# A dilated gated convolution on one core: the lower half of M3 split over taps 2 apart, gates of six classes, joint S and D differences

## The chip, the core and the metric

The kernel runs on one core of a Trainium2 chip. A core has a matrix engine (PE, its weight loads shown as PEld), a vector engine (DVE), a scalar engine (ACT), GpSimd (POOL) and a sync engine (SP) that here issues transfers. Each works off its own queue in order, and semaphores hold an instruction until what it needs is there. The metric is the device time of one execution in microseconds (us): 306.66 before, the median of 3 runs (306.5 to 307.13).

## The reference

x is 2 x 16000 x 144, w is 15 x 144 x 288, w_o is 144 x 144, all bf16. A causal convolution of 15 taps, 2 steps apart, gives 288 columns; tanh of the first 144 times the sigmoid of the others goes through w_o.

```python
def reference(x, w, w_o):
    B, T, D = x.shape
    K = w.shape[0]
    dil = 2
    pad = (K - 1) * dil
    xp = jnp.pad(x, ((0, 0), (pad, 0), (0, 0)))
    h = jnp.einsum('btc,cd->btd', xp[:, pad:pad + T, :], w[0])
    for i in range(1, K):
        off = pad - i * dil
        h = h + jnp.einsum('btc,cd->btd', xp[:, off:off + T, :], w[i])
    f = h[..., :D]; g = h[..., D:]
    z = jnp.tanh(f) * sigmoid(g)
    return z @ w_o
```

## The kernel before

**Tiling.** Both batches lie behind one another as 32,032 steps, cut into ten blocks of 3072 and one of 1536. A block holds two planes (even and odd steps) of 128 channels in `xn`; the 16 channels that are left, for eight taps, come through a buffer in DRAM (`rs`) as `rx`. A block of 3072 is worked in two units (r = 0 and 1), the last one in a single unit: 21 units. A unit covers 12 classes of 128 output positions; `y` holds 12 x 288 sums, `zs` their 12 x 144 gated values.

**A fast convolution.** The 15 taps are not summed one by one. From x, DVE forms sums and differences 8 positions apart (`S`, `D`) and 16 apart (`E`), and of these differences 4 and 2 apart (`S4`, `D4`, `E4`, `S2`, `D2`, `E2`, and `E42` of E4); `Sr`, `Dr`, `Er` are the same for `rx`. `derive` makes each of them with one subtraction or addition, into a tile of its own. They are the weights that PE loads (`stat` picks 128 positions of one); the taps, and sums of taps made at the start (`G`, `GN`, `H`, `PW`, `PX`, `WN`), are the moving operands of 288 columns. Four products m = 0 to 3 (M0 with S, M1 with D, M2 and M3 with E) are combined to the 12 classes.

**Steps of a unit.** An order written out by hand (the strings FIRST for unit 0, EVEN and ODD in turn for units 1 to 19, FINAL for unit 20) says in which order the steps are issued; each engine gets its own steps in that order, fixed by `K_`. The steps that the change and the prediction name:
- `V.m` (`pe_V`, 2 matmuls) opens a `px` tile of two banks, `Vk.m` copies its first bank to its second on ACT, `Vp.m` adds 2 matmuls to each. `C.m.b` copies a bank of it to a `py` bank.
- `X.m.b` and `Y.m.b` (`pe_A`) add 4 matmuls and one for the rest channels onto those banks, for m = 0 and 1; `tX`, `tY` (ACT, `scaled`) take them to `m0` and `m1`.
- `v.m` (ACT) takes the px bank pair of V.2 or V.3 to `v2` or `v3`.
- `A.2.1`, `A.2.0`, `A.3.1` (`A_common`, 2 matmuls) write one bank, `Ak` copies it to a second bank, `Ap.m.b2.b1` (`A_private`, 3 matmuls) adds to each, `At` (DVE) takes the banks to `y`. A.2.1 lies in a px tile, the other two in py banks.
- The lower half of M3 goes another way: `X.3.0` and `X.3.1` add 3 + 1 matmuls each onto V.3's px tile, and `tX.3` (DVE) takes it.
- On DVE, `P` adds m0 and m1 (once for each half b2), `U` adds v2 to P (once for each half), `u3` takes v3 from the upper half of P, `s` writes m0 - m1.
- Gates: `gt.c`, `gs.c` (ACT, tanh and sigmoid of four classes from class c = 0, 4, 8), `gm.c` (DVE) multiplies them into `zs`. gt.0 and gs.0 run in the next unit.
- `zT` (SP) transposes `zs` by a transfer, `po.g` (6 matmuls of 144 columns) multiplies by w_o, `o.g` (ACT) copies out, `ST` stores. `LD` and `LL` issue loads.
- S, D, S4, D4, S2, D2, Sr and Dr of the next block are made in ODD, the E's of the block in EVEN.

**Buffers.** PSUM holds 2 `px` tiles of two banks, 3 `py` banks and 1 `po` bank. `d_pool` (S and D) has two buffers, `e_pool` one, `zs` two. Line 203 of the profile is every DVE sum, 305 every matmul of `mm`, 448 the gates, 542 the plain copies on ACT, 556 `scaled`, 482 the copies of `o`.

Of the kernel before, what the change touches and what calls it, by code (L numbers as in the profile page):

```python
# [22 lines left out]
):  # L23

# [800 lines left out]
```

## Time and profile before

| what | value |
|---|---|
| the three runs | 306.5, 307.13, 306.66 us |
| the profiled execution | 306.78 us |
| its span, first to last instruction | 305.0 us |
| granted PE clock, mean | 0.996 |
| PE, PEld busy | 295.2, 283.2 us |
| DVE, ACT busy | 281.6, 274.5 us |
| DVE, ACT instructions | 478, 635 |
| moved by DMA | 39.71 MB, mean 130 GB/s |

The span is the time between the first and the last instruction of the profiled execution; the rest of its time lies around it. Busy time is the union of an engine's instructions. In the groups of instructions a row is: source line, engine, operation, out<-in, out<-in (partitions x elements, type), count | busy us, mean ns of one | idle us before them and who ended it. A timeline row is: start, length in us, engine, line, operation, count; an idle time before it stands in brackets. A chain row is: start, length, engine, tile, line, count. The whole chain before is PE for 85%.

### The profile page before, as it was taken

What the parts mean: (1) busy time and instruction counts of PE and PEld (TensorE: products, weight loads), DVE (VectorE), ACT (ScalarE), POOL (GpSimd) and SP (SyncE); (2) the same over time, 40 slices, a digit from 0 to 9 for tenths busy, and PEclk for the clock granted to TensorE, in tenths of its full rate; (3) what the DMA queues carried; (4) which work ended last, traced back from release to release, by engine and by line L of the source; (5) the groups of instructions that cost most, each with busy time, mean ns of one, the idle gap of its engine ahead of it and who ended that gap; (6) DMA issues with size and microseconds to landing.
All of it is one profiled execution on the core that took longest, in us unless ns stands there. A gap on an engine that the chain in (4) does not pass through costs nothing.

```text
span 305.0 us, 6949 instructions
## 1 busy us (share of the span) xinstructions
PE 295.2 (97%) x2613; PEld 283.2 (93%) x2613; DVE 281.6 (92%) x478; ACT 274.5 (90%) x635; POOL 31.1 (10%) x69
## 2 busy tenths in 40 slices
...
GB/s 195 132 90 221 42 155 122 103 122 169 166 62 130 177 149 116 148 207 91 146 210 87 159 133 130 136 131 165 105 163 139 160 66 140 160 36 78 98 89 80
DMA packets 175914, 39.71 MB, mean 130 GB/s; under 512 B 173128, under 2 KB 175688, under 8 KB 175880
## 3 DMA queue, kind: packets, MB, share of 16 engines
...
## 4 chain that ended last, share of the span: by engine, by line
PE 85%; DMA 6%; POOL 4%; DVE 3%; issue 1%; ACT 0%; POOLq 0%; DVEq 0%
PE px L305 47%; PE py L305 28%; PE po L305 10%; DMA rs<-wz 3%; DMA rx<-rs 2%; POOL Wr L284 2%; POOL rs L139 1%; DMA wo_ab<-in_w_o_dram 1%; POOL wo_ab L341 1%; DVE S L203 1%; DVE y L203 0%; PE py L516 0%; DVE D L203 0%; DVE z L203 0%; DVE Dr L203 0%
## 5 line engine op out<-in xcount | busy, mean ns | idle before, releaser
L305 PEld LDWEIGHTS <-E 128*128 128x128 bf16 x756 | 94.7, 141 | 1.3 <-issue 0.3
L305 PEld LDWEIGHTS <-D 128*128 128x128 bf16 x462 | 56.9, 138 | 1.3 <-DVE D L203 0.6
L305 PEld LDWEIGHTS <-S 128*128 128x128 bf16 x462 | 56.6, 138 | 1.4 <-issue 0.7
L305 PE MATMUL px<-H,E 128*128 128x288 bf16 x252 | 44.6, 286 | 0.1
L542 ACT COPY px<-px 128x288 f32<-128x288 f32 x105 | 42.5, 405 | 1.5 <-PE px L305 0.7
L448 ACT ACTIVATE th<-y 128x576 bf16<-128x576 bf16 x62 | 42.9, 692 | 0.9 <-DVE y L203 0.9
L448 ACT ACTIVATE sg<-y 128x576 bf16<-128x576 bf16 x62 | 42.8, 690 | 0.0
L305 PE MATMUL po<-wo_ab,zT 128*128 128x144 bf16 x468 | 42.0, 226 | 0.0
L482 ACT CAST os<-po 128x432 bf16<-128x432 f32 x77 | 40.5, 526 | 0.0
L542 ACT COPY py<-px 128x288 f32<-128x288 f32 x84 | 32.5, 396 | 6.7 <-DVE y L203 4.8
L305 PEld LDWEIGHTS <-zT 128*128 128x128 bf16 x480 | 35.6, 98 | 2.1
L203 DVE TENSOR_TENSOR E<-E 128x1536 bf16<-128x1536 bf16 (+5 forms) x33 | 36.7, 1140 | 0.3
L556 ACT ACTIVATE m<-py 128x288 bf16<-128x288 f32 x84 | 34.1, 421 | 1.1 <-PE py L305 1.1
L556 ACT ACTIVATE m<-px 128x576 bf16<-128x576 f32 x42 | 27.4, 652 | 4.7 <-PE px L305 4.4
L203 DVE TENSOR_TENSOR z<-th,sg 128x576 bf16<-128x576 bf16 x62 | 27.9, 452 | 1.2 <-ACT sg L448 1.2
L542 ACT CAST v<-px 128x576 bf16<-128x576 f32 x42 | 26.8, 637 | 1.7 <-PE px L305 1.5
L305 PE MATMUL px<-G,S 128*128 128x288 bf16 x168 | 27.5, 286 | 0.0
L305 PE MATMUL py<-GN,D 128*128 128x288 bf16 x168 | 27.5, 286 | 0.0
L305 PE MATMUL py<-GN,S 128*128 128x288 bf16 x168 | 27.4, 286 | 0.0
L305 PE MATMUL px<-G,D 128*128 128x288 bf16 x168 | 26.7, 286 | 0.0
L305 PEld LDWEIGHTS <-Er 128*128 128x128 bf16 x168 | 23.9, 142 | 0.2
L305 PE MATMUL py<-Wr,Er 128*128 128x288 bf16 x84 | 24.0, 286 | 0.0
...
## 6 DMA issues: line engine op xcount, KB each, us to landing
...
xn<-in_x_dram SPq DMA_TRANSPOSE x22
```

The lines of the kernel that those rows point to most:

```text
L139: K_(eng.dma_start(out=bass.AP(o.tensor, o.offset, [[8 * CR, n], [1, 8 * CR]]), in_=wz[0:n, 0:8 * CR]))
L203: return K_(nc.vector.tensor_tensor(out=out_, in0=a, in1=b, op=op))
L284: K_(nc.gpsimd.dma_start(out=Wr[CR * k:CR * (k + 1), 2 + t // 8, :], in_=w[t, CM:D, :]))
L305: K_(nc.tensor.matmul(ps, lhsT=l, rhs=r, start=start and k == 0, stop=stop and k == n - 1, skip_group_check=not start))
L341: K_(nc.gpsimd.memset(wo_ab[:], 0.0))
L448: K_(nc.scalar.activation(out=cur["g", c0][k][:, 0:n], in_=cur["y"][:, c0:c0 + n, D * k:D * k + D], func=(ACT.Tanh, ACT.Sigmoid)[k]))
L482: K_(nc.scalar.copy(out=dst, in_=po[:, 0:n * D]))
L542: K_(nc.scalar.copy(out=dst, in_=src))
L556: K_(nc.scalar.activation(out=dst, in_=ps, func=ACT.Copy, scale=0.5))
```

## The change

M3's lower half gets steps like the other three halves of M2 and M3: `A.3.0` (2 matmuls with the new sum `NX` and `WN[5]`) into a px tile, `Ak.3.0`, `Ap.3.0.0` (1 + 1 matmuls), `Ap.3.0.1` (2 + 1), and `At.3.0` takes `P[0]` less the tile. `E42` is made two positions wider (16). `u3q` takes v3 from both halves of P. FIRST and FINAL keep X.3. Gates cover classes 0 to 5 and 6 to 11 (FINAL's own stay at four), so gt.6, gs.6, gm.6 stand for the steps of 4 and 8; gm.6 runs in the next unit. S and D share one tile, likewise S4 with D4 and S2 with D2; in ODD one subtraction makes S4 and D4 (`SD4`) and one S2 and D2 (`SD2`). P and U are one operation for both halves, U and u3q with v2 or v3 read twice (`twice`), but not in FINAL. The `ze` tiles move to a pool of their own, NX is made in FIRST (`wx`). All four orders are written anew.

```diff
     GEO = {"S": (-8, 16), "D": (-8, 16), "E": (-16, 24), "S4": (-8, 12), "D4": (-8, 12), "E4": (-16, 20),
-           "S2": (-4, 6), "D2": (-4, 6), "E2": (-12, 12), "E42": (-12, 14), "Sr": (0, 8), "Dr": (0, 8), "Er": (-8, 16)}
+           "S2": (-4, 6), "D2": (-4, 6), "E2": (-12, 12), "E42": (-14, 16), "Sr": (0, 8), "Dr": (0, 8), "Er": (-8, 16)}
...
+    def half_tile(cur, nm):
+
+        wd = GEO[nm][1]
+        if nm[0] == "E" or nm[-1] == "r":
+            cur[nm] = ((e_pool if nm[0] == "E" else d_pool).tile([P, wd * P], BF16, name=nm), 0)
+        elif nm not in cur:
+            t_ = d_pool.tile([P, 2 * wd * P], BF16, name="SD" + nm[1:])
+            cur["S" + nm[1:]], cur["D" + nm[1:]] = (t_, 0), (t_, wd * P)
+        return cur[nm]
...
+        if nm in ("SD2", "SD4"):
+
+            st = int(nm[-1])
+            u0, wd = GEO["S" + nm[-1]]
+            b0, bw = GEO["S"]
+            t_, o = half_tile(cur, "S" + nm[-1])[0], u0 - b0
+            b = cur["S"][0]
+            if big:
+                d_in, d_out = [[bw, 2 * P], [1, wd]], [[1, 2 * P * wd]]
+            else:
+                d_in, d_out = [[bw * P, 2], [1, wd * rw]], [[wd * P, 2], [1, wd * rw]]
+                o, st = o * rw, st * rw
+            tt(sub(t_, 0, d_out), sub(b, o + st, d_in), sub(b, o, d_in), ALU.subtract)
+            return
...
+    def neg_sum():
+        tt(NX[:], WN[:, 4, :], w_all[:, 14, :], ALU.subtract)
...
-    def gate_act(cur, c0, k, n=4):
+    def gate_act(cur, c0, k):
         if cur is None:
             return
+        n = 6 if c0 in (0, 6) else 4
         if k == 0:
-            cur["g", c0] = [g_pool.tile([P, 4, D], BF16, name=nm) for nm in ("th", "sg")] + [n]
+            cur["g", c0] = [g_pool.tile([P, 6, D], BF16, name=nm) for nm in ("th", "sg")] + [n]
         K_(nc.scalar.activation(out=cur["g", c0][k][:, 0:n], in_=cur["y"][:, c0:c0 + n, D * k:D * k + D],
                                 func=(ACT.Tanh, ACT.Sigmoid)[k]))
...
+    def twice(t_):
+
+        return sub(t_, 0, [[0, 2], [1, 2 * D2]])
+
+    def add_P(cur, b2=None):
+
+        k = slice(0, 2) if b2 is None else b2
+        tt(cur["P"][:, k], cur[0, "q"][:, k], cur[1, "q"][:, k], ALU.add)
+
+    def add_U(cur, b2=None):
+
+        if b2 is None:
+            both = [[2 * D2, 2], [1, 2 * D2]]
+            tt(sub(cur["U2"], 0, both), sub(cur["P"], 0, both), twice(cur["v2"]), ALU.add)
+        else:
+            tt(cur["U2"][:, b2], cur["P"][:, b2], cur["v2"][:], ALU.add)
...
+    def sub_v3(cur, both=False):
+
+        if both:
+            p = sub(cur["P"], 0, [[2 * D2, 2], [1, 2 * D2]])
+            tt(p, p, twice(cur["v3"]), ALU.subtract)
+            return
         tt(cur["P"][:, 1], cur["P"][:, 1], cur["v3"][:], ALU.subtract)
...
-    AC = {(2, 1): ("PW", 0), (2, 0): ("PW", 2), (3, 1): ("PX", 0)}
+    AC = {(2, 1): [PW[:, 0, :], PW[:, 1, :]], (2, 0): [PW[:, 2, :], PW[:, 3, :]], (3, 1): [PX[:, 0, :], PX[:, 1, :]],
+          (3, 0): [NX[:], WN[:, 5, :]]}
+
+    AP_ = {(2, 1): ([PW[:, 4, :], PW[:, 5, :]], [w_all[:, 0, :], w_all[:, 1, :]]),
+           (2, 0): ([w_all[:, 6, :], w_all[:, 7, :]], [WN[:, 0, :], WN[:, 1, :]]),
+           (3, 1): ([WN[:, 2, :], WN[:, 3, :]], [w_all[:, 8, :], w_all[:, 9, :]]),
+           (3, 0): ([w_all[:, 14, :]], [WN[:, 4, :], WN[:, 5, :]])}
...
     def A_common(cur, m, b2):
-        wt, k = {"PW": PW, "PX": PX}[AC[m, b2][0]], AC[m, b2][1]
-        if (m, b2) == (2, 1):
+        if (m, b2) in ((2, 1), (3, 0)):
             ps = cur["A", m, b2] = x_bank()
             b0, b1 = ps[:, 0, 0:D2], ps[:, 1, 0:D2]
         else:
             cur["A", m, b2] = (y_bank(), y_bank())
             b0, b1 = (t[:, 0:D2] for t in cur["A", m, b2])
         cur["Ab", m, b2] = (b0, b1)
-        mm(b0, [(stat(cur, "E4", SH[m] - (0 if b2 else 4) - j), wt[:, k + j, :]) for j in range(2)], True)
+        mm(b0, [(stat(cur, "E4", SH[m] - (0 if b2 else 4) - j), wt) for j, wt in enumerate(AC[m, b2])], True)
...
     def A_private(cur, m, b2, b1):
-        jobs = []
-        for j in range(2):
-            if m == 3:
-                wt = w_all[:, 8 + j, :] if b1 else WN[:, 2 + j, :]
-            elif b1:
-                wt = w_all[:, j, :] if b2 else WN[:, j, :]
-            else:
-                wt = PW[:, 4 + j, :] if b2 else w_all[:, 6 + j, :]
-            jobs.append((stat(cur, "E42", SH[m] - (0 if b2 else 4) - j - (0 if b1 else 2)), wt))
+        jobs = [(stat(cur, "E42", SH[m] - (0 if b2 else 4) - j - (0 if b1 else 2)), wt) for j, wt in enumerate(AP_[m, b2][b1])]
         jobs.append((stat(cur, "Er", SH[m] + 2 * b1 + 4 * b2), Wr[:, m, :]))
         mm(cur["Ab", m, b2][b1], jobs, False)
...
         if (m, b2) == (2, 1):
             tt(y[:, 10:12, :], u2[:, 1], cur["A", 2, 1][:, :, 0:D2], ALU.add)
+        elif (m, b2) == (3, 0):
+            tt(y[:, 0:2, :], cur["P"][:, 0], cur["A", 3, 0][:, :, 0:D2], ALU.subtract)
...
     FIRST = """
-        B wn0.0 wn0.1 wd.1 wd.0 wh.1 wh.0 S D S2 D2 S4 E D4 E2 Sr Dr E4 Er E42 w.0 z.9 wt.0 V.0 z.3 z.5 w.1 wt.1 Vk.0 V.1 z.12 z.7
-        w.2 wt.2 Vk.1 Vp.0 C.0.0 w.3 z.1 wt.3 Vp.1 wn w.8 C.0.1 wt.8 Y.0.0.main z.10 z.15 C.1.0 w.9 Y.0.1.main wt.9 X.1.0.main w.4
-        Y.1.0.main wt.4 X.0.1.main Y.0.0.rest tY.0.0 C.1.1 X.0.0.main w.5 X.0.1.rest Y.0.1.rest Y.1.0.rest X.0.0.rest wt.5 tX.0
-        tY.0.1 X.1.0.rest X.1.1 tX.1 w.6 V.2 Vk.2 Y.1.1 tY.1.0 A.2.1 Ak.2.1 tY.1.1 Vp.2 A.2.0 v.2 wt.6 Ak.2.0 Ap.2.1.0 Ap.2.1.1 V.3
-        Vk.3 P.1 s P.0 U.1 At.2.1 U.0 w.7 gt.4 wt.7 Ap.2.0.0 Vp.3 Ap.2.0.1 v.3 gs.4 At.2.0.0 A.3.1 V.0.n Vk.0.n X.3.0 X.3.1 At.2.0.1
-        u3 gm.4 tX.3 Ak.3.1 Vp.0.n Ap.3.1.0 At.3.1.0 Ap.3.1.1 At.3.1.1 gt.8 C.0.0.n gs.8 C.0.1.n
+        B wn0.0 wn0.1 wd.1 wd.0 wh.1 wh.0 S D S2 S4 D2 E D4 E2 Sr Dr E4 Er E42 w.0 wt.0 z.15 V.0 w.1 z.3 z.9 z.1 z.5 V.1 Vk.0 wt.1
+        w.2 Vk.1 wt.2 Vp.0 w.3 Vp.1 z.12 C.0.1 wt.3 w.8 C.0.0 Y.0.1.main X.0.0.main wn wt.8 w.9 z.10 z.7 wt.9 C.1.0 Y.0.0.main w.4
+        X.0.1.main wt.4 X.1.0.main w.5 Y.0.0.rest Y.1.0.main wt.5 tY.0.0 C.1.1 w.6 X.0.0.rest X.0.1.rest Y.1.0.rest X.1.0.rest X.1.1
+        Y.0.1.rest wt.6 tX.0 V.2 tY.1.0 Y.1.1 tX.1 Vk.2 tY.0.1 A.2.1 Vp.2 A.2.0 tY.1.1 Ak.2.1 v.2 Ak.2.0 P U w.7 Ap.2.1.0 V.3 Vk.3
+        wt.7 Ap.2.1.1 Ap.2.0.1 At.2.1 Vp.3 Ap.2.0.0 v.3 V.0.n A.3.1 Vk.0.n X.3.0 X.3.1 s At.2.0.0 At.2.0.1 Ak.3.1 Vp.0.n Ap.3.1.0
+        Ap.3.1.1 gt.6 C.0.0.n wx u3 tX.3 At.3.1.0 C.0.1.n gs.6 At.3.1.1
     """
     EVEN = """
-        B Y.0.0 V.1 X.0.0 po.1 X.0.1 gt.0 tY.0.0 Vk.1 Vp.1 Y.0.1 gs.0 o.1 po.2 C.1.0 Y.1.0 tX.0 C.1.1 o.2 E V.2 X.1.1 X.1.0 tY.0.1
-        Vk.2 tY.1.0 tX.1 gm.8.p Er gm.0 E2 E4 E42 P.1 zT LD Vp.2 v.2 Y.1.1 A.2.1 A.2.0 V.3 po.3 tY.1.1 Ak.2.1 s U.1 P.0 Ap.2.1.0
-        Ap.2.1.1 At.2.1 U.0 Ak.2.0 Vk.3 Vp.3 o.3 gt.4 v.3 gs.4 u3 Ap.2.0.0 Ap.2.0.1 At.2.0.0 A.3.1 V.0.n Vk.0.n X.3.1 X.3.0 At.2.0.1
-        gm.4 tX.3 Ak.3.1 Vp.0.n Ap.3.1.0 Ap.3.1.1 At.3.1.0 At.3.1.1 ST LL po.0 gt.8 C.0.0.n C.0.1.n o.0 gs.8
+        B Y.0.0 V.1 Vk.1 tY.0.0 gt.0 X.0.1 X.0.0 Vp.1 po.1 Y.0.1 C.1.0 tX.0 C.1.1 E Y.1.0 X.1.1 V.2 X.1.0 o.1 tY.1.0 gs.0 tY.0.1 Vk.2
+        tX.1 Y.1.1 Er E4 E2 gm.6.p A.2.0 Vp.2 po.2 A.2.1 gm.0 E42 zT LD tY.1.1 P Ak.2.0 v.2 Ak.2.1 U A.3.1 Ap.2.0.0 V.3 Ap.2.1.1
+        Ap.2.1.0 At.2.0.0 At.2.1 s Vk.3 o.2 Vp.3 v.3 po.3 Ap.2.0.1 A.3.0 V.0.n At.2.0.1 u3q Ak.3.1 o.3 Vk.0.n Ak.3.0 gt.6 ST LL
+        Ap.3.1.1 Ap.3.1.0 Vp.0.n Ap.3.0.0 Ap.3.0.1 po.0 At.3.1.0 At.3.1.1 At.3.0 C.0.0.n C.0.1.n gs.6 o.0
     """
     ODD = """
-        B D Y.0.0 X.0.1 po.1 V.1 X.0.0 gt.0 Vk.1 tY.0.0 D2 Vp.1 Y.0.1 tX.0 C.1.0 V.2 Y.1.0 C.1.1 gs.0 o.1 tY.0.1 tY.1.0 Vk.2 Dr
-        gm.8.p X.1.0 X.1.1 Y.1.1 A.2.0 tX.1 tY.1.1 Ak.2.0 Vp.2 v.2 A.2.1 po.2 Ap.2.0.1 Ak.2.1 V.3 Ap.2.1.0 Ap.2.1.1 S D4 S4 gm.0 Sr
-        zT LD P.1 P.0 s o.2 Vk.3 Vp.3 gt.4 v.3 gs.4 U.1 U.0 At.2.1 Ap.2.0.0 At.2.0.0 S2 A.3.1 V.0.n po.3 Vk.0.n X.3.0 X.3.1 Vp.0.n
-        gm.4 At.2.0.1 u3 Ak.3.1 o.3 Ap.3.1.0 Ap.3.1.1 gt.8 ST LL po.0 tX.3 At.3.1.0 At.3.1.1 C.0.0.n gs.8 C.0.1.n o.0
+        B D Y.0.0 X.0.0 X.0.1 V.1 Y.0.1 gt.0 Vk.1 tX.0 tY.0.0 Vp.1 po.1 C.1.0 C.1.1 V.2 Y.1.0 gs.0 Vk.2 o.1 tY.0.1 S Dr X.1.1 X.1.0
+        Y.1.1 Vp.2 tY.1.0 tX.1 tY.1.1 v.2 po.2 A.2.1 A.2.0 Ak.2.1 Ak.2.0 o.2 A.3.1 V.3 Ap.2.1.0 Vk.3 Ap.2.1.1 Ap.2.0.0 Vp.3 Ap.2.0.1
+        Sr SD4 gm.0 SD2 gm.6.p zT LD P U At.2.1 At.2.0.0 A.3.0 po.3 v.3 Ak.3.0 Ak.3.1 V.0.n Ap.3.0.1 s At.2.0.1 u3q Vk.0.n o.3 gt.6
+        ST LL Ap.3.1.0 Ap.3.0.0 Vp.0.n Ap.3.1.1 po.0 At.3.1.0 At.3.0 At.3.1.1 C.0.0.n C.0.1.n gs.6 o.0
     """
...
     FINAL = """
-        B V.1 Y.0.0 Vk.1 gt.0 X.0.1 po.1 Vp.1 gs.0 tY.0.0 C.1.0 X.0.0 Y.0.1 Y.1.0 tX.0 C.1.1 tY.1.0 o.1 E V.2 X.1.0 X.1.1 tY.0.1 Vk.2
-        tX.1 po.2 o.2 E4 E2 E42 gm.8.p gm.0 Er Vp.2 v.2 Y.1.1 A.2.1 tY.1.1 Ak.2.1 A.2.0 V.3 po.3 Vk.3 P.1 s.1 Ap.2.1.1 Ap.2.1.0 Vp.3
-        U.1 s.0 P.0 U.0 o.3 Ak.2.0 Ap.2.0.0 gt.4 v.3 gs.4 At.2.1 At.2.0.0 Ap.2.0.1 At.2.0.1 gt.8 zT q.0 A.3.1 Ak.3.1 gs.8 X.3.0 X.3.1
-        ev.p0.V gm.4 u3 eB tX.3 q.1 Ap.3.1.0 At.3.1.0 gm.8 Ap.3.1.1 At.3.1.1 x6 eT.A eT.B ev.p1.A gp.0.2.1 gp.0.2.0 mh.0 ec.A eT.C
-        gp.2.1.0 gp.2.1.1 gp.3.1.1 gp.3.1.0 mh.1 ec.B e3.4 eT.D e3.7 ec.C ev.p2.A ev.p3.A e3.10 e2.0 ec.D ev.c4.V ev.c7.A ev.c10.A
-        e2.2 ev.c0.V ev.c2.A ST sp.0 sp.1 s4 LD s0
+        B V.1 Y.0.0 X.0.1 Y.0.1 Vk.1 Vp.1 X.0.0 gt.0 tY.0.0 C.1.0 tY.0.1 tX.0 C.1.1 po.1 Y.1.0 gs.0 tY.1.0 E V.2 X.1.0 X.1.1 Y.1.1
+        o.1 Vk.2 tX.1 tY.1.1 E4 E2 Er Vp.2 v.2 A.2.1 A.2.0 po.2 Ak.2.0 V.3 Ak.2.1 Vk.3 E42 gm.6.p gm.0 Ap.2.0.0 Ap.2.1.0 Vp.3
+        Ap.2.1.1 s.1 P.1 s.0 P.0 gt.4 o.2 v.3 U.1 U.0 At.2.0.0 At.2.1 Ap.2.0.1 po.3 A.3.1 X.3.1 X.3.0 gs.4 o.3 Ak.3.1 At.2.0.1 gt.8
+        gm.4 u3 tX.3 eB gs.8 Ap.3.1.0 At.3.1.0 zT LD q.0 Ap.3.1.1 ev.p0.V At.3.1.1 x6 q.1 eT.A gp.0.2.1 gp.2.1.1 gp.0.2.0 gp.2.1.0
+        gp.3.1.0 gp.3.1.1 ev.p1.A gm.8 eT.B mh.0 eT.C ec.A mh.1 ec.B eT.D e3.4 e3.7 ev.p2.V ec.C ev.p3.A ec.D ev.c4.V ev.c7.A e3.10
+        e2.0 e2.2 ev.c10.A ev.c2.A ev.c0.A ST sp.0 sp.1 s4 s0
     """
```

`AP_` gives the same weights as the old code for the old three halves; `stat` and the rest of `derive` add the offset of the half tile. The orders name `P`, `U`, `u3q`, `SD2`, `SD4`, `wx` without change to `step` beyond their entries.

More of the change, by code (lines that the diff above doesn't have):

```diff
@@ L71 @@
     g_pool = ctx.enter_context(tc.tile_pool(name="g", bufs=2))
+    ze_pool = ctx.enter_context(tc.tile_pool(name="ze", bufs=1))
     zt_pool = ctx.enter_context(tc.tile_pool(name="zt", bufs=2))
@@ L245, in derive @@
             x_ = x_[:].rearrange("p e c -> p (e c)")
-        o = t_[:, 0:wd * rw]
+        o = t_[:, t0:t0 + wd * rw]
         if big:
@@ L257, in stat @@
         blk, r = cur["blk"], cur["r"]
-        t_ = blk[nm]
+        t_, t0 = blk[nm]
         k = u - u0
@@ L263, in stat @@
             rw = 2 * (BTOK[blk["bi"]] // 48)
-            return t_[:, k * rw:(k + 2) * rw]
-        return t_[:].rearrange("p (n j) -> p n j", j=wd)[:, :, k + r]
+            return t_[:, t0 + k * rw:t0 + (k + 2) * rw]
+        return t_[:, t0:t0 + wd * P].rearrange("p (n j) -> p n j", j=wd)[:, :, k + r]
     ident = const.tile([P, P], BF16)
@@ L294 @@
     PX = const.tile([CM, 2, D2], BF16)
+    NX = const.tile([CM, D2], BF16)
     def x_bank():
@@ L637, in end_step @@
             c["os"] = os_pool.tile([P, NCL, D], BF16, name="os")
-            c["g", 0] = [g_pool.tile([P, 4, D], BF16, name=nm) for nm in ("th", "sg")] + [4]
+            c["g", 0] = [g_pool.tile([P, 6, D], BF16, name=nm) for nm in ("th", "sg")] + [4]
         elif op == "gp":
```

24 lines of the change are left out of this document (9 added, 15 removed).

## The prediction

> **What bounds the kernel now.** First the busy times, then the same in stretches of 10 us (columns: PE, PEld, DVE, ACT, POOL busy, clock, DMA share, GB/s):
>
> ```profile
> PE 295.2 (97%) x2613; PEld 283.2 (93%) x2613; DVE 281.6 (92%) x478; ACT 274.5 (90%) x635; POOL 31.1 (10%) x69
> ...
> 150.00:160.00 10.00, 10.00 (x92) 9.95 (x91) 9.78 (x17) 9.49 (x23) 0.00 (x0) 1.00 0.97 180
> ```
>
> Three engines look full, PE wholly so, at full clock. Busy time does not tell which one sets the pace, so I take the distance between starts. From the chain of waits, then the timeline:
>
> ```profile
> 126.61 1.96 PE px L305 x16
> ...
> 153.17 1.96 PE px L305 x16
> ```
> ```profile
> 156.32 0.54 PE L305 MATMUL po<-wo_ab,zT 128*128 128x144 bf16 x6
> ...
> 156.69 0.41 PE L305 MATMUL px<-PW,E 128*128 128x288 bf16 x2
> ```
>
> The same place of an even unit comes back after 26.56 us, the time of two units (one EVEN, one ODD). 1.96/16 = 0.1225 us is the step of a matmul of 288 columns; (156.69 - 156.32)/6 = 0.062 that of one of 144. The code gives a unit 96 wide matmuls (V 8, Vp 16, Y 20, X 28, A 6, Ap 18) and 24 narrow: 96 x 0.1225 + 24 x 0.062 = 13.24 us, twice 26.48. So PE stands still for 0.08 us in 26.56: its queue sets the pace in units 1 to 20.
>
> DVE is less full than 98%. From its timeline:
>
> ```profile
> 148.65 1.75 DVE L203 TENSOR_TENSOR E<-xn 128x3072 bf16<-128x3072 bf16 x1
> 150.32 0.45 DVE L203 TENSOR_TENSOR z<-th,sg 128x576 bf16<-128x576 bf16 x1
> 150.69 1.22 DVE L203 TENSOR_TENSOR Er<-rx 128x2048 bf16<-128x2048 bf16 x1
> ```
>
> A queued instruction starts about 0.08 us before the end of the one ahead (148.65 + 1.75 - 150.32). ACT does the same by about 0.10 (a v copy at 158.12 takes 0.64, the next gate starts at 158.66).
>
> **The change, part by part.** Rows used (busy, mean ns of one):
>
> ```profile
> L448 ACT ACTIVATE th<-y 128x576 bf16<-128x576 bf16 x62 | 42.9, 692 | 0.9 <-DVE y L203 0.9
> L542 ACT COPY px<-px 128x288 f32<-128x288 f32 x105 | 42.5, 405 | 1.5 <-PE px L305 0.7
> L203 DVE TENSOR_TENSOR z<-th,sg 128x576 bf16<-128x576 bf16 x62 | 27.9, 452 | 1.2 <-ACT sg L448 1.2
> L203 DVE TENSOR_TENSOR E<-xn 128x3072 bf16<-128x3072 bf16 x10 | 17.5, 1752 | 0.0
> L203 DVE TENSOR_TENSOR y<-m,m 128x1152 bf16<-128x1152 bf16 x20 | 15.1, 753 | 1.2 <-ACT m L556 0.2
> L203 DVE TENSOR_TENSOR E<-E 128x1536 bf16<-128x1536 bf16 x10 | 9.8, 983 | 0.0
> L203 DVE TENSOR_TENSOR S<-S 128x1536 bf16<-128x1536 bf16 x10 | 9.5, 950 | 0.0
> L203 DVE TENSOR_TENSOR S<-S 128x768 bf16<-128x768 bf16 x11 | 7.1, 643 | 0.0
> ```
>
> *PE.* X.3.0 and X.3.1 (2 x 4 matmuls) go; A.3.0 (2), Ap.3.0.0 (2) and Ap.3.0.1 (3) come: 8 - 7 = 1 wide matmul less, in EVEN and ODD alone (FIRST and FINAL keep X.3), so in 19 units: 19 x 0.1225 = **2.33 us** on the bounding queue.
>
> *ACT per unit.* Six gates of 0.69 (4.15) become four over 864 elements. None is in the trace; from 144, 288 and 576 elements (305, 434, 692 ns) the slope is 0.9 ns per element, so 0.94 each, 3.76 in all; bounds 0.90 and 1.04 (1.5 x 0.692). New: Ak.3.0, a copy of 0.405. Net +0.02, and one instruction less to overlap (+0.10): 29 instructions that fill 12.0 us of 13.28 (durations 14.9 less 29 x 0.10) become 12.1 of a unit of 13.12. Hidden under PE.
>
> *DVE per pair of units.* S4 and D4: 2 x 0.950 become one of 3072 elements, 1.752: -0.15. S2 and D2: 2 x 0.644 become 1536 in runs of 6, 0.983: -0.31. E42 grows from 1792 to 2048 elements, 1.093 to 1.220: +0.13. z: six of 0.452 become four of 0.604 (row GN of 864): -0.30. P and U: 0.904 become 0.753 each, four times: -0.60. u3 takes both halves, 0.454 to 0.753, twice: +0.60. Sum -0.63 in durations; but 8 instructions fewer lose 8 x 0.08 = 0.64 of overlap. Nothing: about 25.4 us (durations 28.9 less 43 x 0.08) before and after, against 26.56 before and 26.24 after.
>
> Joint U and joint u3 read v2 or v3 twice through a step of 0. No row has such an operand. Lower bound 0.753 (1152 elements); upper 1.35, the element rate of y<-P,px (576 in 750 ns) doubled. I take 0.753: like that row, all operands are two-byte with neighbours side by side.
> [...]
>
> *Queues.* SP and POOL issue the same transfers in the same order. zT in ODD waits for gm.6.p: from the start of the unit 0.6 (end of the last y) + S, D 2.28 + Dr, Sr 1.21 + SD4 1.67 + two z 1.04 + SD2 0.90 = 7.7 us, where z was complete at 6.4 (168.04 against the unit's 161.7). po.0 reads it at 12.75.
>
> *px banks.* Two tiles, until now five takers in a unit (V.1, V.2, A.2.1, V.3, V.0.n), now six: A.3.0 waits for At.2.1 (DVE), the next V.1 for At.3.0. Places on an unstalled PE queue, counted in matmuls: ODD A.3.0 at 10.05, At.2.1 ends 0.6 + the 7.1 to the second z + P, U 1.34 + 0.75 = 9.8. EVEN: A.3.0 at 10.42; At.2.1 follows Ap.2.1.0 (its end 9.4) and ends 10.14. Room 0.25 and 0.28. E42 ends 7.4 into EVEN, Ap.2.0.0 loads it at 7.7. Cost nothing, with 0.3 us of cover.
>
> *Head.* FIRST has the same matmuls. Joint P and U save DVE 0.13, NX adds one 128x288 (0.3, late), E42 +0.13, one z moves to unit 1: -0.2 or so, while unit 1 of before stands still for 1.06 us (from 29.04 to 42.23, less 96 x 0.1225 and one po). I take 0, bounds -1.1 (all of that filled) and +0.7 (Dr, which waits for rx to 31.6, now has Sr, SD4 and SD2 behind it). *Tail.* Same matmuls; two last os copies change engine: 0, bounds -0.3 and +0.3.
>
> **Sum.** -2.33 on PE. Stalls were 0.04 a unit; with cover down to 0.3 I let them grow by 0.02: +0.4. Head and tail 0. So -1.95. The profiled execution took 306.78 (span 305.0 and 1.78 around it), 0.12 over the median: 306.78 - 1.95 - 0.12 = **304.7 us**.
>
> **Rivals.**
>
> 1. *px bank* (slower). At.2.1 comes late each unit, A.3.0 and all PE work behind it stand. The head of before shows this wait, at V.0.n:
>
> ```profile
> 39.41 0.41 PE L305 MATMUL px<-H,S 128*128 128x288 bf16 x2 [0.35 <-DVE y L203]
> ```
>
> At 0.35 in every unit: 19 x 0.35 = +6.65, less 2.33: 311.0. It decides once At.2.1 is later than the room of 0.25 by more than 0.12, the matmul saved. For: DVE's free time falls from 1.1 to 0.8 us a pair, and U now waits for both halves. Against: y<-m,m and, in ODD, S2 no longer run ahead of At.2.1.
>
> 2. *Gate in front of the copies* (no change). gt.0 of six classes (0.25 longer) stands ahead of C.1.0, tX.0 and C.1.1 in EVEN; adding ACT's steps, C.1.1 ends at 4.1 and X.1.1, which overwrites what it copies, comes at 4.17. Room 0.1. A wait of 0.23 per EVEN unit eats the gain (10 x 0.23): 306.7. Against: ACT has 1 us a unit to catch up.
>
> 3. *zT late in ODD* (slower). From 7.7 to 12.75 are 5.0 us, before 6.4; 5.8 (36.02 to 41.85) is the shortest seen. DMA after the issue at 168.11, in 40 slices from 165 to 176:
>
> ```profile
> DMA  0000000000000001999999997799299999999996
> GB/s 0 0 0 0 0 0 0 0 0 0 0 0 0 0 0 32 213 215 204 220 214 219 171 175 114 158 244 215 20 202 287 281 278 149 101 196 291 288 103 38
> ```
>
> Data flows 1 us after the issue; 0.46 MB at 210 GB/s are 2.2: landed after some 3.4. Late by 0.6 in ten ODD units: 10 x 0.6 - 2.33 = +3.7: 310.3.
>
> 4. *Repeated operand at half rate* (slower). U and u3 at 1.35: +2.4 per pair, DVE needs 27.8 and paces: 9.5 x (27.8 - 26.56) = +11.8: 318.5.
>
> **How the numbers follow.** Forecast 0.75, px bank 0.09, gates 0.09, zT 0.04, half rate 0.03. By less than 0.2% (0.6 us) nothing can be told from no change. Faster 0.75, same 0.09, slower 0.16. The forecast's own range: 304.7 - 1.1 (head) = 303.6 to 306.0 (stalls of 0.07 more a unit). The range takes in the gates' case and a mild px wait (half of saved matmul and room lost): **303.6 to 307.2**; beyond it stay 0.16 above and a few hundredths below.
>
> **What would show it.** Right: the pair at 26.2 to 26.35 us; 19 matmuls fewer; U and P at 0.75; gates of 864 at 0.94; joint differences at 1.75 and 0.98; no PE idle before A.3.0 and X.1.1. Wrong: PE px idle <-DVE y at A.3.0 (rival 1), <-ACT at X.1.1 (2), po <-DMA zT (3), U at 1.35 (4), or unit 1 longer than 13.2 us.

## The result, and the profile after

The changed kernel takes 309.84 us, the median of 6 runs (309.07 to 310.33), against 306.91 for the kernel before on the same chip (6 runs, 306.5 to 307.29): a ratio of 1.0091 [1.0074, 1.0108], slower by 0.9%. The profiled execution took 309.88 with a span of 308.1, at a granted PE clock of 0.995; before it was 306.78, 305.0 and 0.996, so the clock explains nothing.

The busy times of the changed kernel, then the first 10 us of the same stretch as before (columns as before), then the chain of waits at an even unit:

```profile
PE 296.0 (96%) x2594; PEld 281.6 (91%) x2594; DVE 282.4 (92%) x399; ACT 272.8 (89%) x614; POOL 32.2 (10%) x69
```
```profile
150.00:160.00 10.00, 10.00 (x93) 9.89 (x90) 9.79 (x12) 9.55 (x23) 0.00 (x0) 1.00 1.18 141
```
```profile
124.32 1.96 PE px L331 x16
...
151.17 1.96 PE px L331 x16
...
177.83 1.96 PE px L331 x16
```

The matmuls are 2613 - 2594 = 19 fewer, as the change says. Busy times say nothing of the loss: PE reads 100% in that window, because a matmul's row is modelled as 0.28 to 0.29 long while the next one starts 0.12 after it (the PE rows further down), and so covers a short wait in front of the next. The distance between starts shows it: a pair of units took 26.56 us and should have come down to about 26.3; here one takes 26.85 and the next 26.66.

The groups of instructions that answer to the rows of before, and the one that the change adds on PE:

```profile
L478 ACT ACTIVATE th<-y 128x864 bf16<-128x864 bf16 x40 | 37.7, 943 | 0.0
...
L205 DVE TENSOR_TENSOR SD<-SD 128x3072 bf16<-128x3072 bf16 x9 | 15.7, 1750 | 0.0
L205 DVE TENSOR_TENSOR U<-P,v 128x1152 bf16<-128x1152 bf16 x20 | 15.2, 759 | 2.1
L205 DVE TENSOR_TENSOR P<-m,m 128x1152 bf16<-128x1152 bf16 x20 | 15.1, 757 | 0.8 <-ACT m L586 0.8
...
L331 PE MATMUL px<-NX,E 128*128 128x288 bf16 x19 | 5.4, 283 | 0.8 <-DVE y L205 0.8
```

These durations are what was forecast: gates 0.94, the joint difference of S4 and D4 1.75, the joint U 0.76. Only the last row is new: the first matmul of A.3.0 has idle time before it, put down to DVE writing `y`.

To see all waits of PE, also those under a modelled end, I take for each matmul the start of the one ahead plus its step (0.1225 or 0.062) and call what is left a wait. Summed by stretch (us; the last column is the best version, E9 below):

| stretch | before | after | E9 |
|---|---|---|---|
| to the start of unit 1 | 29.04 | 28.65 | 28.96 |
| unit 1 | 13.19 | 13.94 | 13.21 |
| units 2 to 19 | 239.03 | 240.88 | 238.10 |
| unit 20 to the last matmul | 16.28 | 16.91 | 16.88 |
| after the last matmul | 7.44 | 7.73 | 7.19 |
| span | 304.98 | 308.11 | 304.34 |

In units 2 to 19 the saved matmuls are worth 18 x 0.1225 = 2.2 us, and 4.05 us more of waits came in (the difference of the two sums); the largest are A.3.0 1.97 (1.19 in ODD, 0.78 in EVEN: 0.11 a unit), one po.0 0.76, Y.1.0 in ODD 0.56 (0.06 each time), Vp.0.n once 0.23, Y.0.0 0.19, Ap.2.0.0 0.20 and smaller ones. Before, the only one of note was 0.20 at Vp.1. The other losses are unit 1 (+0.75) and the last unit with what follows it (+0.92); the start came 0.39 earlier. All the kernels from here on have the same FIRST, and in their profiles unit 1 starts between 28.38 and 29.21, so this 0.39 is no more than executions differ by.

Now one EVEN unit of the changed kernel, first DVE's timeline from the joint P on, then PE's around A.3.0:

```profile
158.08 0.75 DVE L205 TENSOR_TENSOR P<-m,m 128x1152 bf16<-128x1152 bf16 x1
158.94 0.76 DVE L205 TENSOR_TENSOR U<-P,v 128x1152 bf16<-128x1152 bf16 x1
159.80 0.46 DVE L205 TENSOR_TENSOR y<-U,py 128x288 bf16<-128x288 bf16 x1
160.17 0.75 DVE L205 TENSOR_TENSOR y<-U,px 128x576 bf16<-128x576 bf16 x1
160.84 0.75 DVE L205 TENSOR_TENSOR y<-m,m 128x1152 bf16<-128x1152 bf16 x1
161.50 0.45 DVE L205 TENSOR_TENSOR y<-U,py 128x288 bf16<-128x288 bf16 x1
```
```profile
160.50 0.41 PE L331 MATMUL py<-WN,E 128*128 128x288 bf16 x2
160.74 0.29 PE L331 MATMUL py<-Wr,Er 128*128 128x288 bf16 x1
160.97 0.28 PE L331 MATMUL px<-NX,E 128*128 128x288 bf16 x1
161.09 0.28 PE L331 MATMUL px<-WN,E 128*128 128x288 bf16 x1
```

At.2.1 (`y<-U,px`) ends at 160.17 + 0.75 = 160.92 and A.3.0's first matmul (`NX`) starts at 160.97; by the step of the matmul ahead it would have started at 160.74 + 0.12 = 160.86. That is the px wait of rival 1, at 0.11 us. And the DVE rows show where the time is: U starts 0.86 after P and `y<-U,py` 0.86 after U, each behind the end of what it reads (v2, which U reads too, was done at 158.43). Instructions that read nothing of the one ahead follow at duration less 0.08 (160.17, 160.84, 161.50: steps of 0.67 and 0.66).

### The profile page after: what moved, and what is told of

It is laid out like the page before. It is cut to its first block, busy times and chain, and to the rows that moved or that the text cites. A ratio compares the mean times of both kernels' runs of the same rounds, so it can differ in the third digit from the quotient of the medians.

```text
span 308.1 us, 6789 instructions
## 1 busy us (share of the span) xinstructions
PE 296.0 (96%) x2594; PEld 281.6 (91%) x2594; DVE 282.4 (92%) x399; ACT 272.8 (89%) x614; POOL 32.2 (10%) x69
## 3 DMA queue, kind: packets, MB, share of 16 engines
q0 software_dynamic: 1824, 1.15, 2.0%
## 4 chain that ended last, share of the span: by engine, by line
PE 76%; DVE 8%; DMA 6%; POOL 5%; issue 2%; ACT 1%; POOLq 0%; DVEq 0%
PE px L331 42%; PE py L331 25%; PE po L331 9%; POOL rs L141 3%; DVE SD L205 3%; DMA rx<-rs 2%; DMA zT<-z 2%; DVE y L205 2%; DMA rs<-wz 2%; POOL Wr L309 1%; DVE z L205 1%; DVE P L205 1%; DVE U L205 1%; DMA wo_ab<-in_w_o_dram 0%; DVE Sr L205 0%
## 5 line engine op out<-in xcount | busy, mean ns | idle before, releaser
L331 PEld LDWEIGHTS <-SD 128*128 128x128 bf16 x924 | 114.1, 138 | 2.5 <-issue 0.6
L331 PE MATMUL py<-GN,SD 128*128 128x288 bf16 x336 | 54.5, 286 | 0.2 <-ACT py L572 0.2
L331 PE MATMUL px<-G,SD 128*128 128x288 bf16 x336 | 53.5, 286 | 0.0
L331 PE MATMUL px<-H,SD 128*128 128x288 bf16 x252 | 44.6, 286 | 0.1
L478 ACT ACTIVATE sg<-y 128x864 bf16<-128x864 bf16 (+1 forms) x42 | 39.5, 940 | 0.0
L478 ACT ACTIVATE th<-y 128x864 bf16<-128x864 bf16 (+1 forms) x42 | 39.1, 931 | 0.0
L205 DVE TENSOR_TENSOR SD<-SD 128x1536 bf16<-128x1536 bf16 (+2 forms) x24 | 30.3, 1271 | 0.0
L205 DVE TENSOR_TENSOR z<-th,sg 128x864 bf16<-128x864 bf16 (+1 forms) x42 | 24.4, 596 | 3.1 <-ACT sg L478 3.1
L205 DVE TENSOR_TENSOR SD<-xn 128x2048 bf16<-128x2048 bf16 (+1 forms) x22 | 24.8, 1169 | 0.0
L331 PE MATMUL px<-Wr,Er 128*128 128x288 bf16 x84 | 24.0, 286 | 0.0
```

The lines of the kernel that those rows point to most:

```text
L205: return K_(nc.vector.tensor_tensor(out=out_, in0=a, in1=b, op=op))
L331: K_(nc.tensor.matmul(ps, lhsT=l, rhs=r, start=start and k == 0, stop=stop and k == n - 1, skip_group_check=not start))
L478: K_(nc.scalar.activation(out=cur["g", c0][k][:, 0:n], in_=cur["y"][:, c0:c0 + n, D * k:D * k + D], func=(ACT.Tanh, ACT.Sigmoid)[k]))
```

## The experiments

All edit only the written orders; every kernel computes the whole reference. Ratios are to the kernel before, run beside them: 306.36 us for E1 to E4, 306.26 for E5 to E8, 306.41 for E9 and E10. It had taken 306.91 beside the changed kernel, so gains are read from ratios (0.001 is 0.31 us) or from stretches of the profiles, and not from the times alone. Each ratio is uncertain by 0.001 to 0.0017, the difference of two by about 0.002.

**E1, P and U by halves again.** Gates, joint differences, joint u3q and the split of M3 stay.

```diff
 (EVEN)
-        P Ak.2.0 v.2 Ak.2.1 U A.3.1
+        P.0 P.1 Ak.2.0 v.2 Ak.2.1 U.0 U.1 A.3.1
 (ODD)
-        P U At.2.1 At.2.0.0 A.3.0
+        P.1 P.0 U.1 U.0 At.2.1 At.2.0.0 A.3.0
```

> Only change to the changed kernel: in EVEN and ODD, P and U are issued in halves again (P.0 P.1 U.0 U.1 in EVEN, P.1 P.0 U.1 U.0 in ODD), everything else as it is. Theory (a chain of dependent DVE instructions): the joint P, U and At.2.1 each wait for the one before, a step of 0.86 us where independent ones step 0.67, so At.2.1 ends 0.4 us later than counted and A.3.0 waits for its px tile; with halves a foreign half lies between each pair, At.2.1 ends about 0.25 us earlier, the wait at A.3.0 (2.7 us in all) falls below 0.7, and the time falls by 1.5 to 2.3 us to 307.5 to 308.3. Rival (DVE simply has too much to do): four more instructions a unit cost it 0.13 us more, so the waits grow and the time is 310 to 311. Rival (a sixth taker of two px tiles is too many whatever DVE does): 309.8, unchanged.

Measured: 308.04, ratio 1.0053 [1.0040, 1.0065], span 306.38: a gain of 1.2 us by the ratios and 1.73 by the spans of the profiled executions, where 1.5 to 2.3 were expected. The waits at A.3.0 in units 2 to 19 fell from 1.97 to 0.09. The same place of the EVEN unit in E1, DVE and then PE:

```profile
157.07 0.83 DVE L205 TENSOR_TENSOR P<-m,m 128x576 bf16<-128x576 bf16 x2
157.81 0.83 DVE L205 TENSOR_TENSOR U<-P,v 128x576 bf16<-128x576 bf16 x2
158.55 0.46 DVE L205 TENSOR_TENSOR y<-U,py 128x288 bf16<-128x288 bf16 x1
158.94 0.75 DVE L205 TENSOR_TENSOR y<-U,px 128x576 bf16<-128x576 bf16 x1
```
```profile
159.86 0.29 PE L331 MATMUL py<-Wr,Er 128*128 128x288 bf16 x1
159.98 0.29 PE L331 MATMUL px<-NX,E 128*128 128x288 bf16 x1
```

Four half instructions take 158.55 - 157.07 = 1.48 us from P to the first `y`, two joint ones 159.80 - 158.08 = 1.72. With the halves in turn, each instruction has one that it doesn't read between it and its source, and none waits. At.2.1 now ends at 159.69, 0.29 ahead of A.3.0, which follows the matmul ahead at its step of 0.12. What follows: joining P and U made the chain longer by 0.24. P also starts 0.14 later into the unit (7.68 against 7.54 in E1), and with both gone so is the wait at A.3.0.

**E2, zT earlier in ODD.** Both products of gates are put ahead of the last difference.

```diff
-        Sr SD4 gm.0 SD2 gm.6.p zT LD P U
+        Sr gm.6.p SD4 gm.0 zT LD SD2 P U
```

> Only change to the changed kernel: in ODD, gm.6.p goes ahead of SD4, and zT and LD go ahead of SD2, so that zT starts about 0.9 us earlier; At.2.1 comes no earlier and no later. Theory (zT is late only where other transfers are in its way): the wait of 0.76 us at po.0 in unit 5 goes, and 0.2 to 0.9 us are won, 308.9 to 309.6. Rival (zT's landing is set by traffic and not by its issue): 309.8, with a wait of the same size at some po.0.

Measured: 308.61, 1.0072 [1.0059, 1.0085], span 306.95. The wait at po.0 is gone (0.76 to nothing), and A.3.0 in ODD falls from 1.19 to 0.82 (in units 3 and 5, from 0.22 and 0.39 to 0.1). The other runs that leave these products where they were keep a wait at po.0 (E1 0.91, E3 0.84, E7 0.52, E8 0.29); none of those that put them ahead has one. The transfer that was late in the changed kernel, in its chain of waits:

```profile
90.80 5.81 DMA zT<-z
96.61 0.05 issue
96.66 0.55 PE po L331 x6
```

The product that it waits for ends at 90.74, 8.1 us into the unit (forecast 7.7), and it landed 5.8 us after its start, not 3.4. Only in this one of the ten ODD units does po.0 wait; in the others the landing was early enough, and when it came is not seen there.

**E3, the last unit's old order.** FINAL as before, with gm.6.p for gm.8.p.

```diff
-        B V.1 Y.0.0 X.0.1 Y.0.1 Vk.1 Vp.1 X.0.0 gt.0 tY.0.0 C.1.0 tY.0.1 tX.0 C.1.1 po.1 Y.1.0 gs.0 tY.1.0 E
+        B V.1 Y.0.0 Vk.1 gt.0 X.0.1 po.1 Vp.1 gs.0 tY.0.0 C.1.0 X.0.0 Y.0.1 Y.1.0 tX.0 C.1.1 tY.1.0 o.1 E
...
-        ec.B eT.D e3.4 e3.7 ev.p2.V ec.C ev.p3.A ec.D
+        ec.B e3.4 eT.D e3.7 ec.C ev.p2.A ev.p3.A e3.10 e2.0 ec.D
```

> Only change to the changed kernel: FINAL has the order that it had before (with gm.6.p for gm.8.p). Theory: the new FINAL loses 0.6 us in the last unit and 0.3 behind it (the os copy of ev.p2 on DVE in front of zeC, and ACT's next os copy behind it), so the time is 308.7 to 309.2. Rival (the tail is late because unit 19 leaves gates of six classes behind): 309.8.

Measured: 309.03, 1.0081 [1.0068, 1.0094], span 307.47. The time fell into the expected range only because the whole group ran faster: of the 0.9 us expected, 0.3 are seen in the ratio (0.0010, inside the uncertainty) and 0.2 in the profile (unit 20 16.89 against 16.91, behind it 7.55 against 7.73). In the changed kernel the last copies stood like this (DVE's timeline, then ACT's):

```profile
298.38 0.41 DVE L552 COPY zeB<-py 128x512 bf16<-128x512 bf16 x1
298.72 0.59 DVE L514 CAST os<-px 128x432 bf16<-128x432 f32 x1
299.23 0.41 DVE L552 COPY zeC<-py 128x512 bf16<-128x512 bf16 x1
```
```profile
299.34 0.52 ACT L512 CAST os<-px 128x432 bf16<-128x432 f32 x1 [1.04 <-DVE os L514]
```

The `os` copy that moved to DVE stands ahead of `zeC`, which ends at 299.64; e3.10, among PE's last matmuls with w_o, starts behind it at 299.69, 0.25 late, and ACT is idle for 1.04 us. (eT.D, a transpose on PE, starts 0.24 late too, at 298.52, but behind the product `zh`, which DVE ends at 298.47.) In E3 both waits are gone. But a new one came: Y.1.0 waits 0.47, as ACT's timeline of E3 shows.

```profile
284.76 0.95 ACT L478 ACTIVATE th<-y 128x864 bf16<-128x864 bf16 x1
285.59 0.94 ACT L478 ACTIVATE sg<-y 128x864 bf16<-128x864 bf16 x1
286.40 0.42 ACT L586 ACTIVATE m<-py 128x288 bf16<-128x288 f32 x1
286.69 0.44 ACT L572 COPY py<-px 128x288 f32<-128x288 f32 x1
```

The last row is C.1.0, which Y.1.0 builds on: two gates of six classes now stand ahead of it where two of four classes stood, 2 x 0.25 us more (0.94 each against 0.69). So the old order takes one loss away and brings another of about the same size, and this one comes with the gates that unit 19 leaves behind, much as the rival had it.

E3 shows something else too. It leaves unit 1 as it is in the changed kernel, yet unit 1 takes 13.53 in it and not 13.94. DVE's row of Dr there, in the changed kernel and then in E3:

```profile
32.00 0.69 DVE L205 TENSOR_TENSOR Dr<-rx 128x1024 bf16<-128x1024 bf16 x1 [0.42 <-DMA rx<-rs]
```
```profile
31.52 0.69 DVE L205 TENSOR_TENSOR Dr<-rx 128x1024 bf16<-128x1024 bf16 x1
```

Where Dr stands still for `rx`, At.2.1 ends 10.80 us into unit 1 and A.3.0 waits 0.73; where it does not, 10.30 and 0.23. So 0.41 of the 0.75 that unit 1 lost hangs on when `rx` landed in that execution.

**E4, the three together.**

> The three edits together (halves of P and U, zT earlier in ODD, FINAL in its old order). Theory: the gains add up, 1.5 to 2.3 and 0.2 to 0.9 and 0.6 to 1.1, to 305.5 to 307.5, so as fast as the kernel before or a little faster, with one wide matmul less in 19 units showing as a pair of units of 26.35 to 26.5 us. Rivals (DVE too full, or px tiles too few): above 308.5.

Measured: 306.73, 1.0015 [1.0004, 1.0025], span 304.77. The three separate steps are worth 0.0038, 0.0019 and 0.0010 of ratio, 0.0067 in sum; together they give 1.0091 - 1.0015 = 0.0076. Within the uncertainty of 0.002 they add up, and they are most of the loss against the kernel before; the saved matmuls still do not show as a gain. A steady pair of units takes 26.42, as expected. Unit 1 takes 13.21; Dr does not wait for `rx` in this execution.

**E5, E4 without the split of M3.** EVEN and ODD have X.3.0, X.3.1, tX.3 and u3 again.

```diff
 (EVEN)
-        Ap.2.0.1 A.3.0 V.0.n At.2.0.1 u3q Ak.3.1 o.3 Vk.0.n Ak.3.0 gt.6
+        Ap.2.0.1 V.0.n At.2.0.1 u3 Ak.3.1 o.3 Vk.0.n gt.6
-        Vp.0.n Ap.3.0.0 Ap.3.0.1 po.0 At.3.1.0 At.3.1.1 At.3.0
+        Vp.0.n X.3.0 X.3.1 po.0 At.3.1.0 At.3.1.1 tX.3
 (ODD)
-        At.2.0.0 A.3.0 po.3 v.3 Ak.3.0 Ak.3.1 V.0.n Ap.3.0.1 s At.2.0.1 u3q
+        At.2.0.0 po.3 v.3 Ak.3.1 V.0.n X.3.1 s At.2.0.1 u3
-        Ap.3.1.0 Ap.3.0.0 Vp.0.n
+        Ap.3.1.0 X.3.0 Vp.0.n
```

> e4_all with the split of M3's lower half undone in EVEN and ODD: X.3.0 and X.3.1 onto V.3's px tile and tX.3 take the places of Ap.3.0.0, Ap.3.0.1 and At.3.0, A.3.0 and Ak.3.0 go, u3 takes the upper half alone. 19 wide matmuls more, five takers of the px tiles instead of six, one ACT copy a unit less. Theory (once no one waits for px, a matmul less is 0.1225 us less): 1.5 to 2.5 us slower than e4_all, 1.006 to 1.010 of the kernel before. Rival (a sixth taker costs more than the matmul saves): as fast as e4_all or faster.

Measured: 309.97, 1.0118 [1.0104, 1.0132], more than expected. Units 2 to 19 take 241.55 against 238.40 in E4. Of this, 1.86 are not the split's: Ap.3.1.1 in EVEN waits 0.21 nine times, which it does not in E4, where A.3.0 stands ahead of it with two matmuls (0.245). That the copy Ak.3.1 is then not done yet is the likely reason; the profile names none. A steady pair of units takes 26.84, or 26.63 without this wait, against 26.42 in E4: 0.21 for the two matmuls of a pair, where two steps are 0.245. The saved matmul is real and worth about what the sum gave it. The rival is out: with the waits at px gone, the sixth taker does not cost more than the matmul saves.

**E6, a mended order.** E4, with gm.6.p and SD4 ahead of Dr and Sr in ODD, and a FINAL mixed from both: the changed kernel's head, the old tail, q.1 ahead of x6. The ODD lines are against E4, the FINAL lines against the changed kernel.

```diff
 (ODD)
-        tY.0.1 S Dr X.1.1
+        tY.0.1 S gm.6.p SD4 Dr X.1.1
-        Sr gm.6.p SD4 gm.0 zT LD SD2 P.1
+        Sr gm.0 zT LD SD2 P.1
 (FINAL)
-        zT LD q.0 Ap.3.1.1 ev.p0.V At.3.1.1 x6 q.1 eT.A gp.0.2.1 gp.2.1.1
+        zT LD q.0 Ap.3.1.1 ev.p0.V gm.8 At.3.1.1 q.1 x6 eT.A ev.p1.A gp.0.2.1
```

> e4_all with two more edits: in ODD, gm.6.p and SD4 go ahead of Dr and Sr, so that DVE does not stand still for rx in unit 1; FINAL is the changed kernel's up to At.3.1.1 and the old one's behind it (os copies of ev.p2 and ev.c0 on the old engines). Theory: unit 1 wins 0.3 to 0.5 us, the last unit 0.4 to 0.6 against e4_all (no wait of 0.47 at Y.1.0, none at eT.D and e3.10), so 0.996 to 0.9995 of the kernel before. Rival (head and tail hang on rx and on the last stores): 1.0015 as e4_all.

Measured: 307.45, 1.0036 [1.0023, 1.0049]: a miss. Units 2 to 19 take 238.03 (238.40 in E4, which has one wait of 0.27 at A.3.0 that E6 has not), but unit 20 takes 17.95. PE's timeline in unit 20 of E6:

```profile
293.10 0.29 PE L331 MATMUL py<-Wr,Er 128*128 128x288 bf16 x1
294.01 0.54 PE L331 MATMUL po<-wo_ab,zT 128*128 128x144 bf16 x6 [0.62 <-DVE os L514]
```

q.1 (second row) needs the only `po` bank back from DVE's `os` copy of q.0, and x6, which used to run in that time, was behind it. By the step this wait is 0.78 of the 1.07 that unit 20 takes more than in E4; another 0.47 stands before a transpose. Unit 1 stayed at 13.21; as Dr waited for `rx` neither in E4's profiled execution nor in E6's, this tells nothing of that wait.

**E7, filler in front instead of behind.** The changed kernel, with po.3 ahead of A.3.0 in ODD, to give At.2.1 time.

```diff
-        At.2.0.0 A.3.0 po.3 v.3
+        At.2.0.0 po.3 A.3.0 v.3
```

> Only change to the changed kernel: in ODD, po.3 stands ahead of A.3.0 on PE instead of behind it, so A.3.0 comes 0.37 us later on PE; DVE and ACT keep their orders. Theory (PE waits at A.3.0 for the end of At.2.1, 0.1 to 0.7 us, because it has nothing else to do there): the ODD waits at A.3.0 (1.9 us with unit 1) fall below 0.4, EVEN's 0.8 stay; 1.0 to 1.6 us won, 308.2 to 308.8 at the speed of the chip of the first comparison, 1.004 to 1.006 of the kernel before. Rival (DVE is too full and sets the pace): the wait moves to V.0.n or At.3 and nothing is won, 1.009.

Measured: 310.05, 1.0118 [1.0103, 1.0134]: a miss. A.3.0 in ODD no longer waits, but Ap.3.0.1 does, 0.39 in each of nine units (3.50). EVEN's waits at A.3.0, which were to stay, fall from 0.78 to 0.14; why was not followed up. PE's timeline of E7, then ACT's:

```profile
173.51 0.29 PE L331 MATMUL px<-NX,E 128*128 128x288 bf16 x1
173.64 0.29 PE L331 MATMUL px<-WN,E 128*128 128x288 bf16 x1
173.76 0.41 PE L331 MATMUL px<-H,SD 128*128 128x288 bf16 x2
174.39 0.41 PE L331 MATMUL px<-WN,E 128*128 128x288 bf16 x2 [0.23 <-ACT px L572]
```
```profile
173.96 0.38 ACT L572 COPY px<-px 128x288 f32<-128x288 f32 x1 [0.35 <-PE px L331]
```

A.3.0 must be copied to its second bank (Ak.3.0, the ACT row) before Ap.3.0.1 can add to it: from A.3.0's last matmul at 173.64 to 174.39 are 0.75 us, and without po.3 only V.0.n (0.25) lies between. The filler had been covering this; the place had no slack on either side.

**E8, `s` between the joint P and U.** The opposite test: an independent instruction in the chain, so that U never waits for P, but comes later.

```diff
 (EVEN)
-        P Ak.2.0 v.2 Ak.2.1 U
+        P s Ak.2.0 v.2 Ak.2.1 U
 (ODD)
-        P U At.2.1
+        P s U At.2.1
```

(The later `s` goes in both.)

> Only change to the changed kernel: in EVEN and ODD, s (y <- m0 - m1) goes between the joint P and the joint U instead of behind At.2.1. DVE has the same instructions and fewer dependent neighbours, so it is done sooner with all of them (about 0.2 us a unit); but At.2.1 starts 0.48 us later. Theory (what counts is when At.2.1 ends): the wait at A.3.0 grows from 0.1 to about 0.5 us in every unit, 19 x 0.4 = 7 us more, 1.025 to 1.035 of the kernel before. Rival (DVE's total work counts): 1 to 3 us faster than the changed kernel, below 1.006.

Measured: 315.52, 1.0302 [1.0288, 1.0316], as expected. DVE's timeline of E8:

```profile
160.39 0.76 DVE L205 TENSOR_TENSOR P<-m,m 128x1152 bf16<-128x1152 bf16 x1
161.06 0.76 DVE L205 TENSOR_TENSOR y<-m,m 128x1152 bf16<-128x1152 bf16 x1
161.72 0.76 DVE L205 TENSOR_TENSOR U<-P,v 128x1152 bf16<-128x1152 bf16 x1
162.59 0.46 DVE L205 TENSOR_TENSOR y<-U,py 128x288 bf16<-128x288 bf16 x1
```

The three rows of 0.76 have the same shape. `s` follows P at 0.67 and U follows `s` at 0.66, since neither reads the one ahead; `y` follows U at 0.87, since it does. From P to U is now 1.33 instead of 0.86, 0.47 later, and A.3.0 waits 0.57 in seven of the nine ODD units from 3 to 19 (0.95 in unit 7, 0.08 in unit 19) and 0.37 in most EVEN ones. Against the changed kernel (0.10 and 0.11 in most) that is 0.47 and 0.26 more: the wait at A.3.0 is set by when At.2.1 is done.

**E9, the best version.** E4 with E6's ODD, and the old FINAL with one gate moved behind C.1.0.

```diff
 (FINAL)
-        gt.0 X.0.1 po.1 Vp.1 gs.0 tY.0.0 C.1.0 X.0.0
+        gt.0 X.0.1 po.1 Vp.1 tY.0.0 C.1.0 gs.0 X.0.0
```

> e4_all, with gm.6.p and SD4 ahead of Dr and Sr in ODD (as in e6_mend), and in FINAL's old order gs.0 behind C.1.0 instead of ahead of tY.0.0. Theory: the wait of 0.47 us at Y.1.0 in unit 20 is for C.1.0, which stands behind two gates of six classes; it goes, and 0.3 to 0.6 us are won there and 0.3 in units 2 to 19, as e6_mend's units showed: 0.996 to 0.9995 of the kernel before. Rival (gs.0 later makes gm.0 and zT late, as in e6_mend): a wait of 0.3 us or more at q.0 takes its place, 1.000 to 1.003.

Measured: 306.17, 0.9993 [0.9984, 1.0001], span 304.34, at the upper edge of what was expected. It beats the changed kernel and equals the one before; that it is faster than that one isn't shown. Y.1.0 in unit 20 waits no more, but V.2 there now waits 0.43, and the unit still takes 16.88: the wait was moved, not taken away.

**E10, E9 with the joint P and U.** The one edit that E1 undid, now made in the mended order.

> e9_gs with the joint P and U back in EVEN and ODD, nothing else changed. Theory (the dependent chain P, U, At.2.1 is what makes A.3.0 wait): 1.2 to 2.3 us slower than e9_gs, with the waits at A.3.0 back at about 0.1 us a unit. Rival (zT and the tail were the cause, and the halves only came with them): within 0.4 us of e9_gs.

Measured: 308.25, 1.0057 [1.0045, 1.0069]: 2.1 us over E9. A.3.0 waits 1.72 in units 2 to 19 (EVEN 0.88, ODD 0.84; in E9 nothing), Ap.2.0.0 0.23, and unit 1 takes 0.22 more. In units 2 to 19 the joint P and U cost 1.82 us here (239.92 against 238.10) and 1.80 without the other two edits (240.88 against 239.08 in E1), so their cost does not hang on the other faults.

## Why the prediction was wrong

The forecast of 304.7 was -2.33 on PE, +0.4 of stalls and nothing at head and tail. The span rose by 3.13 instead of falling by 1.95. Of the 5.08 between them, 3.65 are stalls in units 2 to 19, 0.92 the last unit and what follows, and the rest the head. The largest single part is the step named below: 2.17 (A.3.0 1.97 and Ap.2.0.0 0.20; E10 brings both back). Put right alone (E1), it leaves the kernel at 1.0053, and even E9, at 0.9993, is short of the 0.9936 forecast.

- *The matmuls, -2.33*: right. There are 19 fewer in the trace, and the two of a pair are worth 0.21 in E5.
- *Durations*: right but for one, the repeated operand too: forecast 753 ns, from a row that repeats none; measured 759 for U and 751 for u3q, where rival 4 had 1350, so rival 4 is out. The 1536-element difference (SD2) was put too low: 1.12 to 1.15 in its places, 0.98 forecast.
- *"P, U 1.34", and with it "Room 0.25 and 0.28" and "Cost nothing"*: **the step that failed.** It took 0.08 of overlap after every instruction. U reads P and At.2.1 reads U; each such step is 0.86, not 0.67. (In EVEN At.2.0.0 stands ahead of At.2.1 and is the one that starts 0.86 after U.) In ODD At.2.1 ends 10.2 us into the unit (9.8 forecast; 0.3 of the difference is the chain, 0.1 the second z, at 7.8 for 7.7), in EVEN 10.5 (10.14), and the room is gone. E1, E8 and E10 show it. The mechanism was rival 1's, given 0.09; but at 0.11 a unit, not 0.35, and alone it would have eaten nearly all of the saved matmuls (1.97 of 2.2).

The trace of before held a warning. This is DVE's timeline there, in the last unit:

```profile
289.11 0.45 DVE L203 TENSOR_TENSOR y<-m,m 128x576 bf16<-128x576 bf16 x1
289.48 0.45 DVE L203 TENSOR_TENSOR P<-m,m 128x576 bf16<-128x576 bf16 x1
289.97 0.46 DVE L203 TENSOR_TENSOR U<-P,v 128x576 bf16<-128x576 bf16 x1
```

P follows an instruction that it does not need at 0.37, but U follows the P that it reads at 0.49. These 0.12, twice, are 0.24: nearly the whole room of 0.25, had the row been read for this. For the joint operations it is 0.19, twice. The old halves avoided it by standing in turn with other work.

- *"Against: y<-m,m and, in ODD, S2 no longer run ahead of At.2.1"*: true of y<-m,m, and it did not help, as the places had counted that already. It is wrong of S2: in the old ODD S2 stands behind At.2.1, and in the new one SD2 (1.13 us) stands ahead of it.
- *Stalls +0.02 a unit*: 0.22 measured (4.05 in 18 units). Half of it is the step above. The rest is the 0.76 at po.0 and small waits whose causes were not followed up; of these, 0.06 at Y.1.0 in each ODD unit and 0.23 at one Vp.0.n stay in E9.
- *zT landing 3.4, rival 3*: the direction right, the size off both ways: 5.8 in the worst unit and a wait of 0.76, but one unit of ten late rather than all.
- *Gates ahead of copies, rival 2*: not at X.1.1 in EVEN, where no steady wait stands; it is seen in unit 20 when FINAL has the old order (E3).
- *Head 0, bounds -1.1 to +0.7*: the start of unit 1 came 0.39 earlier and unit 1 lost 0.75, +0.36 in sum, inside the bounds. The reason given for the upper bound, Dr waiting for `rx` with Sr, SD4 and SD2 behind it, did come about in the profiled execution and is 0.41 of the 0.75 (E3 against the changed kernel). Of the rest, 0.22 is what the joint P and U cost unit 1 in E10.
- *Tail 0, bounds -0.3 and +0.3*: +0.92. The term named the two `os` copies but not what is queued behind them: `zeC`, and with it e3.10 on PE. But this is not the main part: with the old order back (E3), 0.61 stay in unit 20 and 0.11 behind it. What the term left out is that unit 19 now leaves gates of six classes to the last unit, which no term has.

Fewer instructions on DVE were no gain here: their count fell from 478 to 399 and the busy time stayed (281.6 and 282.4 us); in the chain to A.3.0 four half instructions in turn were faster than two joint ones by 0.24 us (E1), and E10 with the joint ones took 2.1 us longer than E9.

Open: why the start behind a source is 0.04 after its end for 576 elements in the trace of before, and 0.11 for 1152 here; what makes Y.1.0 wait 0.06 in each ODD unit; and whether a FINAL exists that hides the gates of six classes from unit 19, which might win back the 0.6 us that E9 loses in unit 20 (those of E3, E6 and E9 don't, and no run with the change has gates of four classes there).
